# Start addresses of the streamed weight slices: 32 bytes past a 128-byte boundary instead of on it

## The chip, the core and the metric

The kernel runs on one NeuronCore of a Trainium2 chip. The metric is device time in microseconds of one execution, from its start to its end on the chip. TensorE multiplies a stationary tile (loaded by a weight load, PEld in the profile) with a moving tile that is streamed through it (PE); VectorE (DVE), ScalarE (ACT) and GpSimd (POOL) prepare tiles and empty PSUM; SyncE (SP) issues all DMAs of this kernel in one fixed order.

## The reference, cut to what matters

```
scores = scale * q @ k.T            # 4 batches, 12 heads, 448 rows, 64 per head; causal mask
x  = softmax(scores) @ v            # gathered to 4 x 448 x 768
u  = x + real(fft(fft(x, axis=1), axis=2))
un = (u - mean(u)) / sqrt(var(u) + 1e-6)
out = u + relu(un @ w_ch1) @ w_ch2  # 768 -> 3072 -> 768
```

The inputs are float32. The two products at the end, `un @ w_ch1` and `relu(..) @ w_ch2`, are what the change bears on.

## The kernel before

The program has three stages that overlap at their borders. In the first, to about 214 us, attention runs pair of heads by pair of heads (`attend`: scores at lines 593 and 600, transposes of the probabilities at 667, the product with v at 677), and the Fourier transform of each finished batch is done as matrix products (`dft`: 735 and 752). All of these are float32 matmuls, and each record of them spends two TensorE cycles on a column.

In the second stage (`f1`, line 1034) the first product is computed, and in the third (`window`, line 1204) the second. Both split each float32 operand in a high and a low part of type float32r and add three products (high by high, high by low, low by high); a Strassen-like scheme makes seven block products of what would be eight. Every matmul of line 1034 has a stationary slice of `w1` (128 columns) and a moving tile with 448 columns; there are 1512. Every matmul of line 1204 has a stationary slice of `w1` (which now holds parts of the hidden layer, 128 columns) and a moving weight slice `wa` or `wb` with 384 columns; there are 1764. Each matmul has a weight load of its own.

The moving tiles of the first product are `ue..` and `0...` for the first group of two batches (g = 0) and `1...` for the second (g = 1), 756 matmuls for each group. The slices `wa` and `wb` are 17 tiles each, 3,072 bytes in a partition. They are filled by ACT, DVE and POOL from split weights, or, for six of the twelve chunks, fetched by DMA (`fetch`, line 1147) from a copy in memory that was made earlier.

What runs after what is written out by hand: `RUN` is a list of all units of work, and each engine's queue takes its units in that order, SP's DMAs included. Tiles of a pool that is opened later reuse the bytes of pools that are closed; a tile waits for the last users of the bytes that it overlaps.

Where the tiles lie follows from the pools. On the left side stand `const` (it holds `w1`), `U` (`ue..`), and above them at different times `A1`, or `E0` and `E2` (`0...`), or `F` in the place of `E2` (`wa`). On the right side, from the top down, stand `top` and below it `Q` and `A2` (the first stage), or `L` (`1...`), or `G` in the place of `L` (`wb` and the sums `acc`). `top` and `gap` are tiles that nothing reads or writes; they only take up bytes. Below, the residue of a tile is its start address in a partition, in bytes, modulo 128. All sizes and inner offsets of the tiles of lines 1034 and 1204 are multiples of 128 bytes, so the residue of a tile is that of everything read from it.

Of the kernel before, what the change touches and what calls it, by code (L numbers as in the profile page):

```python
# [9 lines left out]
F32 = mybir.dt.float32  # L10
# [408 lines left out]
def tile_kernel(ctx, tc, qk, vv, w1, w2, cc, cd, cs, out):  # L419
    nc = tc.nc if tc else None  # L420
    T = {}
# [875 lines left out]
    pools = {}  # L1297

    def pool(stack, name, **kw):
        pools[name] = stack.enter_context(tc.tile_pool(name=name, bufs=1, reuse_waits="tile", **kw))  # L1300

    pool(ctx, "const")
    pool(ctx, "top", side="right")
    T["top"] = pools["top"].tile([128, 24], F32, tag="top", name="top", bufs=1)
    pool(ctx, "U")
    T["gap"] = pools["U"].tile([128, 16], F32, tag="gap", name="gap", bufs=1)
    pool(ctx, "P", space=PSUM)
# [11 lines left out]
    with tc.manual_schedule():  # L1319
        for u in seq:  # L1320
            for key in u["new"]:
                if key in T:
                    continue
                where, shape, dtype, _ = SH[key[0]]
                for k in (*BELOW.get(where, ()), where):
                    if k not in pools:
                        for old in AFTER[k]:
                            stacks[old].close()
                        pool(stacks[k], k, side="right" if k in "LG" else "left")
                if where == "P":  # L1330
                    T[key] = T["psum"][:, plan.bank[key]]
                else:
                    T[key] = pools[where].tile(
                        shape, dtype, tag=f"{key[0]}.{plan.buf[key]}" if key in plan.buf else key[0], name=key[0], bufs=1)
            u["fn"](*([u["eng"]] if u["many"] else []))
# [80 lines left out]
```

## Time and profile before

| | |
|---|---|
| median of three runs | 849.24 us (848.95 to 849.96) |
| the profiled execution | 849.51 us, of which the span from first to last instruction is 847.7 us |
| PE busy | 840.2 us, 99% of the span |
| DVE, ACT, POOL busy | 711.7, 556.2, 472.9 us |
| granted TensorE clock | 1.00 from first to last instruction |

A matmul's record is longer than the time that it costs, since the next one starts while the last is still draining: a matmul of line 1204 has a mean length of 336 ns, but 1050 of them with `wa` are busy for 208.3 us together. What a matmul costs is therefore read from the starts of rows that follow each other in the timeline, divided by the number of matmuls of the earlier row.

### The profile page before, as it was taken

What the parts mean: (1) busy time and instruction counts of PE and PEld (TensorE: products, weight loads), DVE (VectorE), ACT (ScalarE), POOL (GpSimd) and SP (SyncE); (2) the same over time, 40 slices, a digit from 0 to 9 for tenths busy, and PEclk for the clock granted to TensorE, in tenths of its full rate; (3) what the DMA queues carried; (4) which work ended last, traced back from release to release, by engine and by line L of the source; (5) the groups of instructions that cost most, each with busy time, mean ns of one, the idle gap of its engine ahead of it and who ended that gap; (6) DMA issues with size and microseconds to landing.
All of it is one profiled execution on the core that took longest, in us unless ns stands there. A gap on an engine that the chain in (4) does not pass through costs nothing.

```text
span 847.7 us, 15801 instructions
## 1 busy us (share of the span) xinstructions
PE 840.2 (99%) x5407; PEld 755.7 (89%) x5407; DVE 711.7 (84%) x1300; ACT 556.2 (66%) x1148; POOL 472.9 (56%) x509
## 2 busy tenths in 40 slices
PE   8999999999999999999999999999999999999998
PEld 5777678677888899999999999999999999999998
DVE  6889998989999998768888669889978989978654
ACT  7988999989897978667867567665636333222221
POOL 2655766566351234555432346483797865876672
PEclk9999999999999999999999999999999999999999
DMA  8526746755886678877877777556355494354442
GB/s 270 203 73 201 226 159 237 245 174 165 232 256 212 232 252 298 284 255 255 265 262 250 263 244 235 186 194 208 94 186 188 145 308 143 113 183 143 131 140 102
DMA packets 121792, 174.03 MB, mean 205 GB/s; under 512 B 21744, under 2 KB 98800, under 8 KB 121712
## 3 DMA queue, kind: packets, MB, share of 16 engines
q1 hardware_dynamic: 121712, 173.03, 63.1%
q8 instruction: 42, 0.69, 0.4%
q14 instruction: 38, 0.31, 0.1%
HBM read 112.83 MB, written 60.16 MB: 204 GB/s over the span
## 4 chain that ended last, share of the span: by engine, by line
PE 90%; DVE 4%; DMA 2%; ACT 2%; issue 1%; POOL 0%; SPq 0%; DVEq 0%; ACTq 0%
PE psum L1204 35%; PE psum L1034 31%; PE psum L600 6%; PE psum L677 5%; PE psum L667 5%; PE psum L735 3%; PE psum L593 1%; PE psum L752 1%; PE psum L778 1%; PE psum L831 1%; DMA raw<-in_qk_dram 1%; DMA us<-und 1%; DVE w L896 1%; DMA w<-in_w_dram 0%; DVE us L902 0%
## 5 line engine op out<-in xcount | busy, mean ns | idle before, releaser
L1204 PE MATMUL psum<-wa,w 128*128 128x384 f32 x1050 | 208.3, 336 | 0.0
L1204 PEld LDWEIGHTS psum<-wa,w 128*128 128x128 f32 x1050 | 184.1, 188 | 0.9 <-DVE w L896 0.2
L1204 PE MATMUL psum<-wb,w 128*128 128x384 f32 x714 | 149.7, 337 | 0.2
L1204 PEld LDWEIGHTS psum<-wb,w 128*128 128x128 f32 x714 | 125.8, 188 | 1.3 <-issue 0.4
L1034 PE MATMUL psum<-0t,w 128*128 128x448 f32 x432 | 106.3, 366 | 0.0
L1034 PE MATMUL psum<-1t,w 128*128 128x448 f32 x432 | 103.6, 363 | 0.0
L896 POOL TENSOR_TENSOR w<-ws,w 128x384 fp32r<-128x384 f32 x58 | 67.1, 1162 | 59.6 <-ACT w L487 46.2
L870 ACT ACTIVATE w<-w 128x768 int8<-128x768 f32 x48 | 94.5, 1968 | 0.7
L487 ACT CAST w<-us 128x384 fp32r<-128x384 f32 x77 | 38.5, 513 | 80.9 <-PE psum L1204 34.6
L621 ACT ACTIVATE p<-psum,mn 128x256 f32<-128x256 f32 (+3 forms) x168 | 83.5, 530 | 9.9 <-DVE mn L613 9.3
L1034 PEld LDWEIGHTS psum<-1t,w 128*128 128x128 f32 x432 | 80.7, 187 | 6.2 <-ACT c L487 0.4
L1034 PEld LDWEIGHTS psum<-0t,w 128*128 128x128 f32 x432 | 80.1, 188 | 6.4 <-DVE c L1060 0.4
L487 ACT CAST w<-ws 128x384 fp32r<-128x384 f32 x86 | 44.3, 519 | 47.5 <-PE psum L1204 25.9
L1220 DVE TENSOR_TENSOR acc<-psum,acc 128x384 f32<-128x384 f32 x96 | 50.8, 548 | 23.0 <-PE psum L1204 22.8
L613 DVE TENSOR_REDUCE mn<-psum 128x1 f32<-128x448 f32 (+3 forms) x96 | 61.9, 664 | 6.7 <-PE psum L600 5.0
L600 PE MATMUL psum<-raw,qs 64*128 64x384 f32 (+3 forms) x336 | 66.0, 430 | 1.0 <-DVE qs L568 1.0
L896 POOL TENSOR_TENSOR w<-us,w 128x384 fp32r<-128x384 f32 x40 | 46.9, 1175 | 31.1 <-ACT w L487 16.9
L880 DVE SCALAR_TENSOR_TENSOR w<-w,w 128x768 uint32<-128x768 uint32 x48 | 53.0, 1105 | 3.0 <-ACT w L870 2.4
L1034 PE MATMUL psum<-ue,w 128*128 128x448 f32 x216 | 54.3, 367 | 0.3 <-ACT c L1068 0.3
L1060 DVE TENSOR_TENSOR c<-psum,c 128x448 f32<-128x448 f32 x69 | 42.3, 617 | 13.5 <-PE psum L1034 7.9
L667 PEld LDWEIGHTS psum<-cst,p 128*128 128x128 f32 x384 | 42.7, 141 | 11.1 <-issue 3.9
L655 POOL TENSOR_TENSOR p<-p,ri 128x128 f32<-128x128 f32 (+3 forms) x61 | 37.4, 632 | 26.5 <-DVE ri L633 21.5
(198 smaller groups left out, 1862.3 us busy)
## 6 DMA issues: line engine op xcount, KB each, us to landing
w<-in_w_dram SPq DMA_DIRECT2D x48, 768.0 KB, 4.8
h<-c SPq DMA_DIRECT2D x93, 224.0 KB, 2.7
w<-us SPq DMA_DIRECT2D x84, 192.0 KB, 2.9
raw<-in_qk_dram SPq DMA_DIRECT2D x23, 480.0 KB, 5.2
us<-h SPq DMA_DIRECT2D x56, 192.0 KB, 3.2
c<-h SPq DMA_DIRECT2D x56, 192.0 KB, 3.5
wa<-w SPq DMA_DIRECT2D x23, 384.0 KB, 4.8
wb<-w SPq DMA_DIRECT2D x19, 384.0 KB, 5.7
```

Of the source, the lines that this page charges most:

```text
L487: nc.scalar.copy(out=out, in_=in_)
L600: nc.tensor.matmul(out=T[ps][:, at[r]:at[r] + n], lhsT=T[qs][s, q0:q0 + 128], rhs=T[raw][s, QW:QW + n], start=False, stop=y == len(rows) - ...
L613: nc.vector.tensor_reduce(out=z, in_=x, axis=AX, op=ALU.min)
L621: nc.scalar.activation(out=T[pb][:, PO[rr]:PO[rr] + n], in_=T[ps][:, c0:c0 + n], func=ACTF.Exp, scale=-1.0, bias=T[mn][:, rr:rr + 1], accu ...
L667: nc.tensor.transpose(T[ps][:, 128 * k:128 * k + 128], T[pb][:, e:e + 128], T["cst", 0][:, 0:128])
L677: nc.tensor.matmul(out=T[xps][64 * h:64 * h + 64, q0:q0 + w], lhsT=T[v][:, c, h * D:(h + 1) * D], rhs=T[pa][:, s0 + h * sd:s0 + h * sd + w ...
L870: nc.scalar.activation(out=T[w].bitcast(I8)[:, :, 3], in_=T[w][:, :, 1].bitcast(F32), func=ACTF.Prelu, scale=SIGN_SCALE, alpha=SIGN_ALPHA)
L880: nc.vector.scalar_tensor_tensor(out=T[w32], in0=T[w32], scalar=3, in1=T[w][:, :, int(join)], op0=ALU.logical_shift_left, op1=ALU.bitwise_or)
L896: (nc.gpsimd if eng == "G" else nc.vector).tensor_tensor(out=lo(), in0=src(), in1=hi(), op=ALU.subtract)
L1034: nc.tensor.matmul(out=T[ps][:, 0:S], lhsT=w[:, a, t], rhs=T[us[t]][:, b], start=first and k == 0, stop=last and k == 8, skip_group_check= ...
L1204: nc.tensor.matmul(out=T[ps][:, 0:384], lhsT=T[hb][:, a, y], rhs=T[z][:, b], start=first and y + v == 0, stop=last and y == n - 1 and v == ...
L1220: nc.vector.tensor_tensor(out=x, in0=T[ps][:, 0:384], in1=x, op=ALU.add)
```

## The change

Two sizes of unused tiles are changed. `top` shrinks from 24 to 16 float32 (96 to 64 bytes), which moves everything on the right side up by 32 bytes; a new unused tile of 8 float32 (32 bytes) stands at the start of pool `F`, which moves `wa` up by 32 bytes.

```diff
     pool(ctx, "top", side="right")
-    T["top"] = pools["top"].tile([128, 24], F32, tag="top", name="top", bufs=1)
+    T["top"] = pools["top"].tile([128, 16], F32, tag="top", name="top", bufs=1)
     pool(ctx, "U")
     T["gap"] = pools["U"].tile([128, 16], F32, tag="gap", name="gap", bufs=1)
...
                         pool(stacks[k], k, side="right" if k in "LG" else "left")
+                        if k == "F":
+                            T["gap", k] = pools[k].tile([128, 8], F32, tag="gap", name="gap", bufs=1)
```

The addresses in the two built programs give these residues:

| pool | tiles | used as | before | after |
|---|---|---|---|---|
| F | `wa` | moving, line 1204 | 0 | 32 |
| G | `wb`, `acc` | moving, line 1204; sums | 0 | 32 |
| L | `1...` | moving, line 1034, g = 1 | 0 | 32 |
| E2, U | `0...`, `ue..` | moving, line 1034, g = 0 | 0 | 0 |
| const | `w1` | stationary, lines 1034 and 1204 | 64 | 64 |
| A2 | `v`, `pa`, `p` | first stage | 0 to 96 | 32 more each |
| Q | `cd`, `f`, `u` and others | first stage | 0 to 96 | 32 more each |

So the 1764 matmuls of line 1204 and 756 of the 1512 of line 1034 get a moving operand at residue 32; the other 756 of line 1034 keep theirs.

The order of the instructions is the same on every engine. One wait is new. The seventh of the `wa` tiles ended, before, on the byte where a tile of `E2` began; moved by 32 bytes it reaches into that tile, and the DMA that fills it waits for the tile's last matmul as well. On SP's queue, at the last fetches before the second product begins (`h` is the hidden layer's copy in memory, `w` on the right of an arrow the copy of the second product's weights), this stands before:

```order
L1147 DMA wa<-w_75 128x768 [waits DMAHW7_49,PE_49]
L1147 DMA wa<-w_75 128x768 [waits DMAHW0_49,PE_49]
L1045 DMA h<-c_5920 128x448 [waits DMAHW1_49,DVE_49]
L1147 DMA wa<-w_75 128x768 [waits DMAHW2_49]
L1147 DMA wa<-w_75 128x768 [waits DMAHW3_49,PE_49]
```

and this after:

```order
L1147 DMA wa<-w_75 128x768 [waits DMAHW7_49,PE_49]
L1147 DMA wa<-w_75 128x768 [waits DMAHW0_49,PE_49]
L1045 DMA h<-c_5920 128x448 [waits DMAHW1_49,DVE_49]
L1147 DMA wa<-w_75 128x768 [waits DMAHW2_49,PE_49]
L1147 DMA wa<-w_75 128x768 [waits DMAHW3_49,PE_49]
```

Nothing moved; the fourth of these DMAs waits for PE too. On PE, the third matmul of a group of three on that `0...` tile signals, where the group after it did.

## Rows read from the trace of the kernel before

**Rows 1.** The page: busy time of the engines, and PE's granted clock.

```profile
PE 840.2 (99%) x5407; PEld 755.7 (89%) x5407; DVE 711.7 (84%) x1300; ACT 556.2 (66%) x1148; POOL 472.9 (56%) x509
...
PEclk9999999999999999999999999999999999999999
```

**Rows 2.** Busy time by stretch, all engines: first product, second product.

```profile
core 0: us, PE busy (x) PEld busy (x) DVE busy (x) ACT busy (x) POOL busy (x), PEclk, DMA share, GB/s
300.00:480.00 180.00, 180.00 (x900) 168.12 (x900) 146.81 (x253) 129.82 (x168) 80.50 (x72) 1.00 0.79 264
560.00:760.00 200.00, 199.85 (x1149) 198.39 (x1147) 173.56 (x280) 85.88 (x161) 144.43 (x119) 1.00 0.54 169
```

**Rows 3.** Timeline of PE, first product: start us, length, instruction, count.

```profile
399.65 0.76 PE L1034 MATMUL psum<-1222_3788,w 128*128 128x448 f32 x3
400.25 0.76 PE L1034 MATMUL psum<-ue,w 128*128 128x448 f32 x3
400.85 0.76 PE L1034 MATMUL psum<-1212_3814,w 128*128 128x448 f32 x3
401.45 0.76 PE L1034 MATMUL psum<-0t,w 128*128 128x448 f32 x3
402.05 0.76 PE L1034 MATMUL psum<-0220_3175,w 128*128 128x448 f32 x3
```

**Rows 4.** Timeline of PE, second product.

```profile
699.68 0.68 PE L1204 MATMUL psum<-wb,w 128*128 128x384 f32 x3
700.20 0.68 PE L1204 MATMUL psum<-wa,w 128*128 128x384 f32 x3
700.72 1.20 PE L1204 MATMUL psum<-wb,w 128*128 128x384 f32 x6
701.76 0.68 PE L1204 MATMUL psum<-wa,w 128*128 128x384 f32 x3
702.28 1.03 PE L1204 MATMUL psum<-wb,w 128*128 128x384 f32 x5
```

**Rows 5.** Timeline of PE, first stage: transposes, then three products with v.

```profile
144.25 1.04 PE L667 MATMUL psum<-cst,p 128*128 128x128 f32 x8
145.12 1.31 PE L831 MATMUL psum<-cst,un 112*128 112x112 f32 x12
...
147.44 1.98 PE L677 MATMUL psum<-pa,v 128*64 128x384 f32 x28
...
154.89 1.98 PE L677 MATMUL psum<-pa,v 128*64 128x384 f32 x28
...
160.72 1.98 PE L677 MATMUL psum<-pa,v 128*64 128x384 f32 x28
```

**Rows 6.** Groups of ACT's casts: mean ns of one stands after the bar.

```profile
L487 ACT CAST w<-ws 128x384 fp32r<-128x384 f32 x86 | 44.3, 519 | 47.5 <-PE psum L1204 25.9 <-DVE ws L902 20.0 <-POOL ws L902 1.1
L487 ACT CAST w<-us 128x384 fp32r<-128x384 f32 x77 | 38.5, 513 | 80.9 <-PE psum L1204 34.6 <-POOL us L902 14.1 <-DVE us L902 10.1
```

**Rows 7.** The DMAs into the slices on the page: KB each, us to landing.

```profile
wa<-w SPq DMA_DIRECT2D x23, 384.0 KB, 4.8
wb<-w SPq DMA_DIRECT2D x19, 384.0 KB, 5.7
```

**Rows 8.** Timeline of PE: last matmuls on the `0...` tile of the new wait.

```profile
487.53 0.83 PE L1034 MATMUL psum<-0t,w 128*128 128x448 f32 x3
488.20 0.76 PE L1034 MATMUL psum<-1t,w 128*128 128x448 f32 x3
```

**Rows 9.** Timeline of SP: the two DMAs, the first of which waits longer after the change.

```profile
502.22 0.97 SPq L1147 DMA_DIRECT2D wa<-w  x2
```

**Rows 10.** Timeline of PE: the first use of the slice that this DMA fills.

```profile
542.97 1.20 PE L1204 MATMUL psum<-wa,w 128*128 128x384 f32 x6
```

## Prediction

> **What bounds the kernel now.** I read the page first: PE is busy for 840.2 of 847.7 us, and the granted clock stands at the top in every slice [rows 1]. That is the level of 2.4 GHz, so a column takes 0.417 ns. Then the stretches: from 300 to 480 us PE is busy for 180.00 of 180 us with 900 matmuls, from 560 to 760 us for 199.85 of 200 us with 1149; DVE is the next with 173.56 us of the second stretch, ACT and POOL stand lower [rows 2]. So in both products PE's own pace sets the time, and nothing that another engine does comes through unless it grows by more than the 15% that DVE has left.
>
> What is PE's pace? In the first product rows of three matmuls follow each other by 0.600 us, 200.0 ns a matmul, whether the moving tile is `ue`, `0...` or `1...` [rows 3]; 900 in 180 us is the same number [rows 2]. In the second product rows of three follow by 0.520 us and the row of six by 1.04, 173.3 ns a matmul for `wa` and `wb` alike [rows 4]; the 1149 in 200 us give 174.1 with the few stops in between. The columns alone would take 448 x 0.417 = 186.7 ns and 384 x 0.417 = 160.0 ns. Both products thus lose the same 13.3 ns for each matmul, the time of 32 columns, whatever its length.
>
> The slower float32 matmuls of the first stage lose far less: eight transposes with 128 columns, at two cycles a column 106.7 ns, start 0.87 us before the next row, 109 ns each [rows 5], a loss of 2.1 ns with a weight load for each as well. So 11.2 ns of the 13.3 belong to streaming at one cycle a column next to a weight load. Whether these 11.2 ns depend on where the operands start is the whole question, since the trace has the pair 0 (moving) and 64 (stationary) in every matmul of lines 1034 and 1204 and no other.
>
> **The change part by part.** A nanosecond on each of the 1764 + 756 = 2520 matmuls that get residue 32 is 2.52 us of time, 0.30%. Nothing covers it: PE has no idle time in those stretches [rows 2].
>
> The moving read of the two products: not shown for residue 32, so it is bounded from the nearest rows. Below, the shift could take away all that is above the loss of the transposes, 11.2 ns x 2520 = -28.2 us. Above, it could double the loss that is there, 13.3 x 2520 = +33.5 us. The rows that are nearest to the value itself say zero. First, the loss is 13.3 ns in both products although their tiles step differently: high and low part of a moving tile lie 1792 bytes apart in the first and 1536 in the second, which is 256 and 0 modulo 512. A loss made by two reads that meet at certain addresses should differ between the two; one that is paid for each swap of the stationary tile does not. Second, the products with v: the three of [rows 5] have `pa` and `v` at residues 64 and 0, 64 and 32, and 32 and 0 in the order of the rows, and all three take 1.98 us for 28 records. There a column has two cycles, so this shows only that no price is attached to residue 32 as such. I take 0 and keep both ends for the range.
>
> The 11.2 ns also have a rule to be weighed. The rows show 173.3 ns for 384 columns [rows 4]. The Trainium skill, TensorE: Matmul & The Clock Gate, section "Back-to-back issue gap", gives N / 2.4 + 2.5 ns for a warm matmul, by which it would be 162.5 ns, and in "Step-by-step: what each phase is for" it says that loading the next weights "doesn't steal SBUF read bandwidth from the running matmul". The rows differ from the first by 10.8 ns, so here the measurement decides; by the second the shift would change nothing, by the first alone it could at most give those 10.8 ns back, 27 us of the sum.
>
> The first stage: all tiles of `A2` and `Q` move by 32 bytes. The three equal rows of the products with v put this at 0 for PE. For the other engines, the casts into `w` read `ws` at residue 0 in 519 ns and `us` at 64 in 513 ns [rows 6], so their price does not follow the residue by more than 1.2%, and DVE, the nearest to PE, has 26 us of cover in 200 [rows 2]. I cost this at 0; without the cover 1.2% of DVE's 711.7 us would be 8.5 us.
>
> The DMAs into `wa` and `wb` now write to an address 32 bytes on: 42 of them, landing in 4.8 and 5.7 us [rows 7]. They are issued far ahead, as the next step shows for one, and half as long again (2.9 us) would stay hidden. The sums `acc` are stored at the end from residue 32; that store is the one with nothing behind it, but 192 KB more or less aligned is a fraction of a microsecond. Taken as 0.
>
> The new wait: the DMA that it holds back is issued at 502.22 us [rows 9], while the matmul that it now waits for is the last of the row that starts at 487.53 us and ends at 488.36 [rows 8]. It is met 13.9 us ahead. Behind it on SP stands the next fetch, which waits for PE already. The slice is first read within the row that starts at 542.97 us [rows 10], 40 us later. Price 0; without that slack it would be a delay of SP's queue by at most the time to the next matmul row.
>
> The sum is 0 against the profiled 849.51 us, which is 847.7 us of span and 1.8 us around it. The median of the runs shown lies 0.27 us lower. I predict 849.3 us.
>
> **The rivals.** *Slower: a stream that starts off its boundary pays for a part of a line.* If TensorE's moving read fetches blocks longer than 32 bytes and a stream that starts 32 bytes into one gets its first or last block late, each matmul pays about the time of the eight float32 columns that 32 bytes hold, 8 x 0.417 = 3.3 ns. That is 2520 x 3.3 = +8.4 us, 857.7 us. It decides from 0.7 ns a matmul on (1.7 us, the 0.2% that a measurement of this kernel can tell from no change). For it: a read at one column a cycle has no slack to hide a late block, unlike the first stage, so the equal rows there do not exclude it. Against it: nothing in the trace shows a block of such a size. Its worst form is the doubled loss, 883 us, which would need each load to meet the stream twice as often.
>
> *Faster: the loss comes from the two reads meeting, and at 32 against 64 they meet less often.* For it: 11.2 ns appear only where the stream has no slack. A change by the same eight columns gives -8.4 us, 840.9 us; all of it 821 us, where DVE with 87% of the stretch [rows 2] would still keep up with a PE that is 6% faster. Against it: the same 32 columns in both products, whatever the steps of the tiles.
>
> *The change does only half of what it says.* It moves 756 tiles of the first product as well, while the loss might hang on one product alone. Then the rivals above shrink to 1764 matmuls, 5.9 us either way. That changes sizes, not signs, and gets no chance of its own.
>
> **How the numbers follow.** No change 0.46, slower by the part of a line or more 0.32, faster 0.22. The forecast is that of the likeliest, 849.3 us, and its own range is 847.6 to 851.0. For eight in ten the range must reach well into both rivals: 836 us is the faster case with 5.3 ns a matmul, 866 us the slower with 6.6 ns, about half of each bound. I leave out about 0.08 below and 0.1 above. The same cases give faster 0.22, same 0.46, slower 0.32.
>
> **What would show it.** In the profile after, the starts of successive rows: 0.520 us for three matmuls of line 1204 and 0.600 us for three of line 1034. If they hold, the pace does not depend on residue 32. If the first is 0.53 and rows with `1...` take 0.61 while `ue` and `0...` stay at 0.60, the slower rival is right, and the `ue` rows are its control, since their addresses stay. If they shrink, the faster one. The products with v should still take 1.98 us for 28. The fetch that waits longer should be issued near 502 us. The prediction is wrong if the stage of attention, up to 214 us, changes by more than a microsecond, since I give nothing to the moved tiles there.

## The result and the profile after

The changed kernel takes 857.03 us (856.21 to 858.2), the kernel before, run beside it, 849.1 us: a ratio of 1.0095, 95% interval 1.0079 to 1.0111. It is 7.9 us slower. That lies inside the range of the prediction, 0.7 us from its slower rival and 7.7 us from the forecast, which was no change. The profiled execution took 858.2 us with a span of 856.4, where before it was 849.51 and 847.7.

The page of the kernel after, beside [rows 1]: PE is busy for 8.7 us more, as much as the span grew, at the same granted clock, and its weight loads for 7.0 us more; no other engine is busy for more than 0.3 us longer.

```profile
PE 848.9 (99%) x5407; PEld 762.7 (89%) x5407; DVE 705.4 (82%) x1300; ACT 556.5 (65%) x1148; POOL 470.9 (55%) x509
...
PEclk9999999999999999999999999999999999999999
```

Busy time by stretch in the kernel after; the columns are those of [rows 2]. In the same 180 us there are 889 matmuls of the first product where there were 900, and in the same 200 us 1134 of the second where there were 1149.

```profile
300.00:480.00 180.00, 180.00 (x889) 166.50 (x889) 144.42 (x250) 130.35 (x167) 80.42 (x72) 1.00 0.79 263
560.00:760.00 200.00, 200.00 (x1134) 199.86 (x1133) 169.06 (x274) 87.03 (x163) 141.34 (x118) 1.00 0.53 166
```

PE's timeline after, second product, to hold beside [rows 4]. Rows of three now follow by 0.53 us and rows of six by 1.06, for `wa` and `wb` alike: 176.7 ns a matmul in place of 173.3.

```profile
700.06 0.69 PE L1204 MATMUL psum<-wa,w 128*128 128x384 f32 x3
700.59 1.22 PE L1204 MATMUL psum<-wb,w 128*128 128x384 f32 x6
701.65 0.69 PE L1204 MATMUL psum<-wa,w 128*128 128x384 f32 x3
702.18 1.22 PE L1204 MATMUL psum<-wb,w 128*128 128x384 f32 x6
```

The first product, beside [rows 3]. The starts of the rows with `1...`, whose tiles moved, are followed 0.61 or 0.62 us later by the next row; those with `0t` and `ue`, which did not move, still by 0.60.

```profile
399.86 0.77 PE L1034 MATMUL psum<-1t,w 128*128 128x448 f32 x3
400.47 0.78 PE L1034 MATMUL psum<-1221_3705,w 128*128 128x448 f32 x3
401.09 0.76 PE L1034 MATMUL psum<-0t,w 128*128 128x448 f32 x3
401.69 0.76 PE L1034 MATMUL psum<-ue,w 128*128 128x448 f32 x3
402.29 0.77 PE L1034 MATMUL psum<-1222_3788,w 128*128 128x448 f32 x3
```

The first stage kept its pace: the products with v take 1.98 us for 28 records as in [rows 5], and the stretch to 214 us has PE busy for 211.91 us with 2025 matmuls, where the kernel before has 211.35 with 2026. In the products with v both operands moved by 32 bytes; in the transposes (line 667) `p` moved and `cst` did not, and their 256 records up to 150 us keep PE busy for 33.20 us in both kernels (the last line shows them after the change).

```profile
147.77 1.98 PE L677 MATMUL psum<-pa,v 128*64 128x384 f32 x28
155.21 1.98 PE L677 MATMUL psum<-pa,v 128*64 128x384 f32 x28
161.05 1.98 PE L677 MATMUL psum<-pa,v 128*64 128x384 f32 x28
...
0.00:150.00 150.00, 33.20 (x256) 28.53 (x256) 1.00 0.59 196
```

### The profile page after: what moved, and what is told of

Read it like the earlier page. It is cut to its first block, busy times and chain, and to the rows that moved or that the text cites. A ratio compares the mean times of both kernels' runs of the same rounds, so it can differ in the third digit from the quotient of the medians.

```text
span 856.4 us, 15802 instructions
## 1 busy us (share of the span) xinstructions
PE 848.9 (99%) x5407; PEld 762.7 (89%) x5407; DVE 705.4 (82%) x1300; ACT 556.5 (65%) x1148; POOL 470.9 (55%) x509
## 4 chain that ended last, share of the span: by engine, by line
PE 82%; DVE 3%; ACT 2%; DMA 1%; issue 1%; DVEq 0%
PE psum L1204 36%; PE psum L1034 32%; PE psum L677 3%; PE psum L600 3%; PE psum L667 3%; PE psum L735 2%; PE psum L752 1%; PE psum L778 1%; ACT p L621 1%; PE psum L593 1%; DMA us<-und 1%; PE psum L831 1%; DMA w<-in_w_dram 0%; DVE w L896 0%; DVE us L902 0%
## 5 line engine op out<-in xcount | busy, mean ns | idle before, releaser
L1204 PE MATMUL psum<-wa,w 128*128 128x384 f32 x1050 | 211.2, 339 | 0.0
L1204 PEld LDWEIGHTS psum<-wa,w 128*128 128x128 f32 x1050 | 187.1, 188 | 0.2
L1204 PE MATMUL psum<-wb,w 128*128 128x384 f32 x714 | 151.6, 339 | 0.0
L1204 PEld LDWEIGHTS psum<-wb,w 128*128 128x128 f32 x714 | 127.8, 188 | 0.2 <-POOL w L896 0.2
L1034 PE MATMUL psum<-1t,w 128*128 128x448 f32 x432 | 105.4, 367 | 0.0
L487 ACT CAST w<-ws 128x384 fp32r<-128x384 f32 x86 | 44.5, 521 | 47.2 <-PE psum L1204 30.1
L896 POOL TENSOR_TENSOR w<-us,w 128x384 fp32r<-128x384 f32 x40 | 46.8, 1172 | 32.5 <-ACT w L487 20.9
L1220 DVE TENSOR_TENSOR ue<-psum,ue 128x384 f32<-128x384 f32 x72 | 38.5, 549 | 16.6 <-PE psum L1204 15.3
```

What stands on the lines that cost most here:

```text
L487: nc.scalar.copy(out=out, in_=in_)
L896: (nc.gpsimd if eng == "G" else nc.vector).tensor_tensor(out=lo(), in0=src(), in1=hi(), op=ALU.subtract)
L1034: nc.tensor.matmul(out=T[ps][:, 0:S], lhsT=w[:, a, t], rhs=T[us[t]][:, b], start=first and k == 0, stop=last and k == 8, skip_group_check= ...
L1204: nc.tensor.matmul(out=T[ps][:, 0:384], lhsT=T[hb][:, a, y], rhs=T[z][:, b], start=first and y + v == 0, stop=last and y == n - 1 and v == ...
L1220: nc.vector.tensor_tensor(out=x, in0=T[ps][:, 0:384], in1=x, op=ALU.add)
```

## The experiments

All kernels are the kernel before with other sizes of unused tiles, which move whole sides by multiples of 32 bytes, unless said otherwise. What a matmul costs is the distance between its start and the next one's, averaged over groups of three with no wait in them; the lost columns are what is left after 448 or 384 columns at 0.417 ns, in columns. I call *distance* the start of the moving tile minus the start of the stationary tile, in bytes; it was 64 modulo 128 (and modulo 256) for every matmul of the kernel before.

The theory that I took first was that of the slower rival: a stream that starts 32 bytes past a boundary pays for them, wherever its partner lies. The rival to it: what counts is the distance.

**The right side alone.**

```diff
-    T["top"] = pools["top"].tile([128, 24], F32, tag="top", name="top", bufs=1)
+    T["top"] = pools["top"].tile([128, 16], F32, tag="top", name="top", bufs=1)
```

> Only the right side moves by 32 bytes: the moving tiles 1... and wb lie at 32 modulo 128, ue, 0... and wa stay at 0, the stationary tiles stay at 64; the wait that the change added is not there. If each matmul pays for where its own moving tile starts, matmuls with wb cost 176.7 ns and those with wa 173.3 in the same windows, rows with 1... about 0.61 us for three and ue 0.60; 714 + 756 matmuls with 3.3 ns more give +4.9 us, 854.0. If it is the added wait, or the transfers into wa, the time stays at 849.1. If a stage as a whole slows down, wa and wb cost the same.

Measured: 853.14 us, ratio 1.005 (1.0035 to 1.0065). In the same windows `wb`, which moved, costs more than `wa`, which did not: in PE's timeline of this kernel a row of six with `wb` is followed after 1.05 us and one of six with `wa` after 1.04, rows of three after 0.53 and 0.52.

```profile
700.30 1.22 PE L1204 MATMUL psum<-wb,w 128*128 128x384 f32 x6
701.35 1.20 PE L1204 MATMUL psum<-wa,w 128*128 128x384 f32 x6
702.39 0.69 PE L1204 MATMUL psum<-wb,w 128*128 128x384 f32 x3
702.92 0.68 PE L1204 MATMUL psum<-wa,w 128*128 128x384 f32 x3
703.44 1.22 PE L1204 MATMUL psum<-wb,w 128*128 128x384 f32 x6
```

Over the whole product `wa` loses 31.4 columns and `wb` 38.5; `1...` loses 43.1 and `0...` and `ue` 33.6. So the cost goes with the tile, not with the stage, the new wait or the transfers into `wa`, which this kernel leaves as they were. `wb` stays a little under the 40 columns that it loses when `wa` has moved too, and the unmoved tiles of the first product lose 1.5 more than before: a matmul's pace also carries something of its neighbours.

**The stationary tiles alone.** `eps`, a small tile ahead of `w1`, is halved, and the gap above grows by as much, so that all moving tiles of the two products stay where they were (`bfc`, `w`, `w32` and `us`, which lie beside `w1`, move along with it).

```diff
-        "eps": ("const", [128, 16], F32, 1),
+        "eps": ("const", [128, 8], F32, 1),
...
-    T["gap"] = pools["U"].tile([128, 16], F32, tag="gap", name="gap", bufs=1)
+    T["gap"] = pools["U"].tile([128, 24], F32, tag="gap", name="gap", bufs=1)
```

> All moving tiles stay at 0, the stationary tiles of both products go from 64 to 32. Theory of the start (a matmul pays for the place where its moving stream starts in a block): 173.3 and 200.0 ns as before, 849.1 us. Theory of the distance (what counts is moving minus stationary modulo 128, 64 before and 96 in the changed kernel): the distance is 96, as in the changed kernel, so 176.7 ns for all 1764 and 203.3 for all 1512, +10.9 us, 860.0.

Measured: 860.02 us, ratio 1.0129 (1.0114 to 1.0145). The stretches of this kernel:

```profile
300.00:480.00 180.00, 180.00 (x878) 164.36 (x877) 142.31 (x245) 128.57 (x164) 80.42 (x72) 1.00 0.77 262
560.00:760.00 200.00, 200.00 (x1133) 199.86 (x1132) 167.78 (x273) 87.69 (x165) 141.01 (x119) 1.00 0.54 167
```

1133 matmuls of the second product in 200 us are the changed kernel's pace, 40.0 columns lost, with every moving tile on its old place at 0. The theory of the start falls here.

**Everything together by 32 bytes.** `eps` grows to 24 and `top` shrinks to 16, so moving tiles go to 32 and stationary tiles to 96.

> Everything moves together by 32 bytes: moving tiles at 32, stationary at 96. Theory of the start: 40 columns lost in all 3276 matmuls, 176.7 and 203.3 ns, 860.0 us. Theory of the distance: it is 64 again, as before, 173.3 and 200.0 ns, 849.1 us.

Measured: 848.92 us, ratio 1.0 (0.999 to 1.0009). Both stretches are back:

```profile
300.00:480.00 180.00, 180.00 (x901) 168.16 (x900) 146.42 (x252) 129.88 (x168) 80.01 (x72) 1.00 0.78 264
560.00:760.00 200.00, 199.89 (x1151) 198.90 (x1150) 173.79 (x280) 85.91 (x161) 143.78 (x119) 1.00 0.54 169
```

Here the moving slices lie at 32 modulo 128, as in the changed kernel, all tiles of the first stage but `cst` have moved, and it costs nothing, since the partner moved along. The two runs together show that the distance decides, and neither place by itself.

**Both at 64.** The gap is left out and `top` has 8 float32: moving tiles at 64, stationary at 64.

> All moving tiles at 64, the stationary tiles at 64. Theory of the start with blocks of 128 bytes: 16 columns more than at 0, 48 lost, 180.0 and 206.7 ns, +21.8 us, 870.9; with blocks of 64 bytes: as at 0, 849.1 us. Theory of the distance: it is 0, a value that no kernel had so far; anything between 0 and 64 lost columns.

Measured: 855.11 us, ratio 1.0064 (1.0048 to 1.0081). This was not one pace but two. In PE's timeline of the second product rows of three with `wa` are followed after 0.52 us, rows of six with `wb` after 1.06:

```profile
701.33 1.22 PE L1204 MATMUL psum<-wb,w 128*128 128x384 f32 x6
702.39 0.68 PE L1204 MATMUL psum<-wa,w 128*128 128x384 f32 x3
702.91 1.22 PE L1204 MATMUL psum<-wb,w 128*128 128x384 f32 x6
703.97 1.20 PE L1204 MATMUL psum<-wa,w 128*128 128x384 f32 x6
```

`wa` loses 32.5 columns, `wb` 40.1. Both are at distance 0 modulo 128; modulo 256 `wa` is at 0 and `wb` at 128. So 128 bytes are not the whole period.

**Both at 0.** `eps` has 32 float32, the gap is left out: moving tiles at 0, stationary at 0.

> Moving at 0, stationary at 0: the distance is 0, as it was with both at 64, where a matmul lost 35.7 columns in the second product and 40.6 in the first and the kernel took 855.1 us. Theory of the distance: the same numbers, 855 us. A theory in which the stationary tile's own place counts (64 good, 32 bad) gives no number for 0, but no reason for just these.

Measured: 854.9 us, ratio 1.005 (1.0034 to 1.0067). The time is the one expected, but not for the reason given: the second product runs at its old pace, 1152 matmuls in 200 us, and the first loses 44.5 columns.

```profile
300.00:480.00 180.00, 180.00 (x875) 163.86 (x874) 141.97 (x244) 128.48 (x164) 80.36 (x72) 1.00 0.78 261
560.00:760.00 200.00, 200.00 (x1152) 199.14 (x1151) 174.95 (x278) 88.19 (x166) 143.53 (x121) 1.00 0.54 169
```

Modulo 256 all of its distances are 0, on both sides, which agrees with `wa` in the run before. (In the first product the run before had 41.3 lost columns at distance 0, where the other side lay at 128, so neighbours are worth some three columns there.) A distance that is as good as 64 for the second product is bad for the first.

**Moving tiles at 96.** The gap has 8 float32, `top` is left out.

> Moving at 96, stationary at 64: the distance is 32, the last of the four steps of 32 bytes. If the loss grows with how far the distance is from 64, on either side, it is as at 96: 40 columns in the second product, 860 us. If instead a stream that is ahead differs from one that is behind, it lies elsewhere, between 32 columns (849) and less (a loss of 6 columns, that of the transposes, would be 818).

Measured: 853.67 us, ratio 1.0048 (1.0033 to 1.0063). Again the two products part: 32.1 columns in the second, 43.3 in the first. Modulo 256 the distance is 32 on the left and 160 on the right, and in the second product both are free.

```profile
300.00:480.00 180.00, 180.00 (x880) 164.50 (x879) 142.53 (x246) 129.27 (x165) 80.79 (x72) 1.00 0.79 262
560.00:760.00 200.00, 199.96 (x1151) 198.86 (x1150) 174.92 (x278) 88.30 (x166) 144.14 (x121) 1.00 0.54 170
```

So the loss is not the same on both sides of 64: in the second product 32 is free, 96 is not.

**64 and 192.** `eps` has 8 float32, `top` is left out, the gap stays: the stationary tiles lie at 32, all moving tiles at 96.

> Stationary tiles at 32, all moving tiles at 96: the distance is 64 modulo 128 everywhere, as before. Modulo 256 it is 64 on the left (ue, 0..., wa) and 192 on the right (1..., wb). Theory of the distance modulo 128: 173.3 and 200.0 ns for all, 849 us. Theory of the distance modulo 256, to which the runs with both at 64 point (there wa at 0 lost 32.5 columns and wb at 128 lost 40.1): the left keeps 32 lost columns, the right has a distance that no kernel had, and differs if 192 is not as good as 64; with 40 columns and more it is 854 and up.

Measured: 852.01 us, ratio 1.0026 (1.0014 to 1.0037). The left side, distance 64, loses 31.7 columns in the second product and 34.7 in the first; the right side, distance 192, 34.5 and 38.5. 192 is not as good as 64 although it is the same modulo 128, and it is better than 96. The effect on the time is smaller than the other ones, but its interval excludes no change.

```profile
300.00:480.00 180.00, 180.00 (x891) 166.94 (x891) 143.97 (x249) 130.50 (x168) 80.15 (x72) 1.00 0.79 263
560.00:760.00 200.00, 200.00 (x1150) 199.08 (x1149) 174.36 (x281) 85.88 (x163) 143.65 (x119) 1.00 0.53 166
```

**Steps of 8 and 16 bytes.** `eps` has 8 float32, `top` and the gap are left out, and five of the eight buffers of `w1` get a pad and a start within it.

```diff
-    pools = {}
+    pools, turn = {}, {}
...
+                    if key[0] == "w1":
+                        n = turn.setdefault(plan.buf[key], len(turn))
+                        if n < 5:
+                            o = (4, 4, 4, 4, 2)[n]
+                            z = pools[where].tile([128, 776], dtype, tag=f"w1.{plan.buf[key]}", name="w1", bufs=1)
+                            T[key] = z[:, o:o + 768].rearrange("p (a t m) -> p a t m", a=2, t=3)
+                            continue
```

> Distances in steps of 8 and 16 bytes in one execution: five of the eight stationary buffers start at 48, 80, 112, 16 and 40 modulo 128, three at 64; ue, 0... and wa lie at 64, 1... and wb at 96. The distances are 0, 16, 24, 32, 48, 56, 80 and 112. Read by pace of the matmuls of each kind, not by the kernel's time, which mixes them. If the loss is smooth around 64, 56 and 80 lie between 32 and 40 columns; if some distance lets the two reads miss each other, its matmuls lose less than 32 columns; if only steps of 32 bytes count, 48 and 56 cost what 32 costs, 80 what 64 costs (32 columns).

Measured, by kind of matmul (the trace's matmuls matched in order with the program's, which gives each its distance modulo 256), in one execution: between 32.6 (distance 32) and 38.0 lost columns (176) in the second product, between 39.0 and 43.0 in the first. 48 costs 36.7 in the second product and 56 35.9, which points to steps below 32 bytes counting too, and they find no distance that costs less than 32 columns. With so many kinds next to each other the neighbours blur the numbers (distance 0 loses 34.6 here, 32.2 in a kernel of its own), so this run only bounds.

**The second product alone.** The change, with an unused tile of 32 bytes at the end of pool `L`, which puts `1...` back to 0.

```diff
-    pools = {}
+    pools, held = {}, []
...
+                    if where == "L":
+                        held.append(key)
+                        if len(held) == 21:
+                            T["gap", "L"] = pools["L"].tile([128, 8], F32, tag="gap", name="gap", bufs=1)
```

> wa and wb at 32, the moving tiles 1... of the first product back at 0 (the first stage stays 32 bytes on): the change to the second product alone. Theory of the distance: 1764 x 3.3 ns, +5.9 us, 855.0 us, 173.3 becomes 176.7 ns and line 1034 stays at 200.0. If half of the changed kernel's loss came from the moved tiles of the first stage or from the wait, it would be 853 or less.

Measured: 854.44 us, ratio 1.0052 (1.0037 to 1.0067), some 4.4 us more than before by the ratio. The pace is the expected one. In the trace the starts of the second product's matmuls are 4.5 us further apart in sum than before, not 5.9, because 1.4 us went into stops: gaps between starts of over 190 ns exceed the pace by 1.7 us in sum before and by 0.3 us here. Line 1204 loses 40.0 columns, line 1034 is back at 32.1, with the new wait, the moved DMAs and the moved first stage still in place.

```profile
300.00:480.00 180.00, 180.00 (x900) 168.18 (x899) 145.41 (x252) 129.49 (x168) 80.30 (x73) 1.00 0.79 264
560.00:760.00 200.00, 200.00 (x1134) 199.86 (x1133) 168.32 (x277) 84.95 (x159) 140.41 (x117) 1.00 0.53 165
```

**Half as many stationary columns**, on the kernel with the right side moved.

```diff
-out=T[ps][:, 0:384], lhsT=T[hb][:, a, y], rhs=T[z][:, b],
+out=T[ps][0:64, 0:384], lhsT=T[hb][:, a, y, 0:64], rhs=T[z][:, b],
```

> As the kernel with the right side alone moved (wa at distance 64, wb at 96), but each matmul of line 1204 has a stationary tile with 64 columns in place of 128, so half of the rows of the second product are left out and its weight loads read half as much. If the lost columns are the reads of the weight load, 32 becomes 16 with wa and 40 some 20 with wb: 166.7 and 168.3 ns. If they are paid for each swap of the stationary tile, whatever its size, wa keeps 173.3 and wb 176.7 ns. Its time is that of a kernel with less of the same work and is read by pace only.

Measured in one execution: 35.3 lost columns with `wa` and 37.4 with `wb`, where the full stationary tile lost 31.4 and 38.5. In 200 us of the second product there are 1145 matmuls, with the full tile 1146, though the weight loads are busy for 153.47 us in place of 199.42 and one of them has a record of 134 ns in place of 188. First the kernel with the right side moved, then this one:

```profile
560.00:760.00 200.00, 200.00 (x1146) 199.42 (x1145) 171.79 (x279) 85.25 (x161) 143.37 (x119) 1.00 0.53 165
L1204 PEld LDWEIGHTS psum<-wa,w 128*128 128x128 f32 x1050 | 184.6, 188 | 0.5 <-ACT acc L487 0.2 <-DVE acc L1220 0.2
...
560.00:760.00 200.00, 200.00 (x1145) 153.47 (x1144) 172.25 (x278) 85.69 (x161) 142.51 (x120) 1.00 0.53 166
L1204 PEld LDWEIGHTS psum<-wa,w 128*64 128x64 f32 x1050 | 140.8, 134 | 42.9 <-ACT acc L487 0.2 <-DVE acc L1220 0.2 <-DVE w L896 0.2
```

The loss did not halve, so it is not the sum of the load's reads, and the pace is not set by how long the load takes. Nor did the two numbers stay: `wa` lost 3.9 more, and the difference between the distances shrank from 7.1 to 2.1 columns. A price of some 32 columns for each swap, with a part on top that depends on what the load reads, would look like this, but the run does not show it, and why `wa` got slower is open.

The distances modulo 256 that whole kernels or whole sides had, and the columns lost:

| distance | second product | first product |
|---|---|---|
| 0 | 32.2 | 44.5 |
| 32 | 32.2 | 42.6 |
| 64 | 32.0 | 32.1 |
| 96 | 40.0 | 44.8 |
| 128 | 40.1 | 40.2 |
| 160 | 32.0 | 44.3 |
| 192 | 34.5 | 38.5 |

(0 is from the kernel with both at 0, 64 from the kernel before, 96 from the one with the stationary tiles moved; the others are one side of a kernel.) Where the two sides differ, the neighbours count too: in the first product 64 gave 33.6 and 34.7 in such kernels, and 0 gave 41.3. So differences of some three columns in the last column say little. Of these seven, 64 is the only one without a price in both products.

## Why the prediction was right or wrong

**What bounds the kernel** was right: PE's own pace. The 8.7 us by which the span grew are PE's 8.7 us. That nothing covers a slower pace was nearly right: some 2 us of it went into stops, as the next sum shows.

**The price per nanosecond** was right: 2520 matmuls, 2.52 us each nanosecond. The second product's 1764 got 3.3 ns each (40.0 in place of 32.0 columns), the 756 with `1...` 4.6 (43.1 in place of 32.1), and the 756 beside them 0.6. Those are 5.9 + 3.5 + 0.5 = 9.9 us. Not all of it comes through. In the two traces the starts within the second product are 4.45 us further apart in sum after the change and those within the first 3.26, together 7.7. The other 2 us went into stops that PE had before: gaps between starts of over 190 ns exceed the pace of the second product by 1.7 us before and by 0.3 after, gaps of over 217 ns that of the first by 6.0 and 5.4. The rest of the 8.7 us of the span lies outside the two products; the medians differ by 7.9.

**The value taken for the moving read** is the step that failed: 0, from two rows. The first argument was that a loss made by two reads meeting should differ between the products, whose steps differ, and that it was 13.3 ns in both. The runs show that both lay on a floor of 32 columns: at five of the six other distances that were tried the products do differ, as with 40.0 against 44.8 at 96 and 32.2 against 44.5 at 0; at 128 they do not. Equal numbers at one point of a curve said nothing about its slope. The second argument, three products with v that cost the same at three pairs of residues [rows 5], was a row of the first stage with two cycles a column; it told of that stage alone, as the text said, and was given more weight than that. So the change was put at nothing, and it cost 3.3 ns with `wa` and `wb` and 4.6 ns with `1...`.

**The rule** that a load of weights "doesn't steal SBUF read bandwidth from the running matmul" (the Trainium skill, TensorE: Matmul & The Clock Gate, section "Step-by-step: what each phase is for") does not hold here when it is read as a rule on time. Moving the stationary tiles by 32 bytes, and no moving tile of the two products, took the second product from 173.3 to 176.7 ns a matmul and the kernel from 849.03 to 860.02 us.

**The slower rival** gave 857.7 us, and 857.03 was measured; its control, `ue` and `0...` near 0.60 us, is what the trace shows. Its price of eight columns is the 8.0 that the second product lost. That the sum came so near is luck: by the paces it would be 9.9 us and not 8.4, as the first product's moved tiles lost 11 columns and not eight, and about that much more went into stops. Its mechanism is wrong: a stream that starts at 32 pays nothing when its partner lies at 96, and pays in full at 0 when its partner lies at 32. **The faster rival** came nearest to the cause, as it let the pace depend on where the two reads start against each other, and had the wrong sign: 64 is already the best distance of those tried. That its gain could be had anywhere was tried at seven distances in steps of 32 bytes and at some between, and none lost less than about 32 columns.

**The other terms**, the wait, the DMAs and the moved first stage, were right at 0: the waiting fetch is issued at 506.02 us in the profile after, where it was 502.22 [rows 9], in the same place of the queue, later as the fetches ahead of it are too, and some 40 us ahead of its first use; and the kernel with everything moved together, in which all tiles of the first stage but `cst` and the targets of all fetches lie 32 bytes on, is as fast as before. That **the loss might hang on one product alone** was considered, and it did not: the second product alone gives a ratio of 1.0052 where the whole change gives 1.0095, so the first product has some two fifths of the loss.

What stays open is the mechanism below the numbers. That the pace depends on the distance between the start addresses of the stationary and the moving operand is shown. That the load and the stream disturb each other in reading, and that it is a matter of which part of the memory each reads at a time, is only argued; the record of a weight load stays at 188 ns in the kernels before and after. Why the first product, with 448 columns and its low part 256 bytes off modulo 512, is free at 64 alone, while the second is free at 0, 32, 64 and 160, was not settled, nor was distance 224 tried.

## What to carry to other kernels

Where matmuls stream one column a cycle with a weight load for each, measure start to start and compare with the columns; then try a few starts of the moving tile against the stationary one, since 32 bytes cost 2% of such a stage here. Move the two apart by unused bytes in a pool, and test both a shift of one and a shift of both: only the pair tells a place from a distance. Here a stage that runs at half that pace told nothing of it.

## What the runs showed of the hardware

A float32r matmul with its own weight load cost its columns plus about 32 more at the best of the distances tried, for 384 and for 448 columns, at the full granted clock. With other distances between the start addresses of the two operands it cost up to 13 columns more (44.8). The same distance modulo 128 was not enough: `wa` at 0 and `wb` at 128 modulo 256 lost 32.5 and 40.1 columns in the same kernel. With a stationary tile half as wide the loss did not halve but stood at 35.3 and 37.4 columns.
